# Spectral units as 28 operations each, emitted at the times of a table, in a single-core spectral and GEGLU kernel

## The chip, the cores and the metric

The kernel runs on one core of one Trainium2 chip. The core has a matrix engine (TensorE, PE in the profile; its weight loads are shown apart as PEld), VectorE (DVE), ScalarE (ACT), GpSimd (POOL) and SyncE (SP), which here issues all DMA transfers. Each engine works through its own list of instructions in order; between engines there are semaphores. The metric is the device time of one execution in microseconds (us), and for a kernel the median of its runs.

## What is computed

The input x is 8192 rows of 448 columns. It goes through two conditioned blocks:

```python
mod = (silu(c) @ w_mod)                      # six rows of 448: sa, ca, ga, sb, cb, gb
h = layernorm(x) * (1 + ca) + sa
x = x + ga * A(h)                            # spectral mixer
h = layernorm(x) * (1 + cb) + sb
x = x + gb * ((gelu(h @ w_gate) * (h @ w_up)) @ w_down)

def A(h):                                    # the transform is along the 8192 rows
    z = rfft(h)                              # 4097 frequencies x 448, as 4 blocks of 112
    h = relu(z @ w1 + b1)                    # complex, per block; relu on real and imaginary part
    o = h @ w2 + b2
    o = softshrink(o, 0.01)                  # real and imaginary part apart
    return irfft(o)
```

The matrix products need more precision than one pass of the matrix engine gives, so operands are split into a high and a low part and three products are added.

## The kernel before, in words

The program has three stretches.

1. **0 to about 80 us.** x is loaded, layer norm statistics are taken, and the first factor of the transform (128 points) runs on PE. Its result td goes to DRAM.
2. **About 80 to 419 us: the spectral stage**, which the change is about. There are 32 *units* (h, bt): h is a half of the columns (224 of 448), bt one of 16 groups of four frequencies. Each unit goes through the same operations, most of them twice (kk or p = 0, 1):
   - `fetch_t` (SP, L347 and L356): the unit's part of td into the tile tr, and for a new bt the factors s2. `split_t`: th on ACT and tl on POOL (helper lines L108 and L110 in the profile).
   - `stage_s2`: 12 matmuls (L378 to L380), zh on ACT (L386), zl on DVE (L387).
   - `stage_m1`: 12 matmuls (L424 to L429), hh on ACT (L441), hl on DVE (L442).
   - `stage_m2`: 12 matmuls (L451 to L456), the threshold t (p = 0 on DVE, L467; p = 1 on ACT, L465), y with four DVE operations (L477 or L479). `split_y`: yh on ACT (L108), yl on POOL (L110).
   - `stage_i1`: 3 matmuls (L508 to L510), us on ACT (L511); after both, two DMA stores into vd (L513).
3. **About 419 us to the end: GEGLU** over 32 chunks of 256 rows, with the second factor of the inverse transform at the start of each. PE is busy all through.

The order in stretch 2 is written out by hand. `step(i)` emits, one after the other: the fetch of unit i+2, s2 of unit i, the split of unit i+1, m2 of unit i-2, i1 of unit i-3, m1 of unit i-1. `step(0)` to `step(30)` follow each other, and `drain` writes out the rest. What an engine does follows this order, so the operations of one stage of one unit stand behind each other on each engine.

Side work for stretch 3 is hung into the steps with `at(i, hook, fn)`: a hook is one of five places in a step (load, pe, act, dve, pool). It loads and reduces modulation rows (`mod_sum`, L640 and L641; `mod_row`, L649), takes norms of the up-projection weights (`squares`, L672; `norms`, L681), sums the down-projection pieces (`down_sums`, L791 to L798), and, from step 18 on, splits gate and up weights into wh and wl (`weights_hi`, L770 to L773; `weights_lo`, L779 and L781) and the first down pieces (`down_hi`, L877; `down_lo`, L881). Short scalar work waits in a list `tiny`; `drip()` emits one entry of it between the operations of a unit.

On-chip tiles rotate: tr, s2, th, tl, t, y and us have two buffers, zh, zl, hh, hl, yh and yl four. Of the matrix engine's eight result banks, two each serve s2 (pa), m1 (pb), m2 (pc) and i1 with side work (pd).

Of the kernel before, what the change touches and what calls it, by code (L numbers as in the profile page):

```python
# [10 lines left out]
F32 = mybir.dt.float32  # L11
# [8 lines left out]
D = 448  # L20
# [18 lines left out]
LAM = 0.01  # L39
EPS = 1e-5  # L40
# [5 lines left out]
def spectral_geglu(ctx, tc, x, wt_in, wgu, wd, cvec, wmod, cf1, cs2, cmi, cgm, out):  # L46
# [290 lines left out]
    with ExitStack() as bctx:  # L337
# [21 lines left out]
        def split_t(h, bt, el=G):  # L359
            raw, s2 = trs.pop((h, bt))  # L360
            th = bp1.tile([128, GB, HC], F16, tag="th", name="th", bufs=2)
            tl = bp1.tile([128, GB, HC], F16, tag="tl", name="tl", bufs=2)
            split(th, tl, raw, el=el)
            tts[(h, bt)] = th, tl, s2

        cnt = {"z": 0, "h": 0}
        ctx_u = {}

        def stage_s2(h, bt):
            tht, tlt, s2 = tts.pop((h, bt))  # L370
            zs = []
            for kk in range(2):
                ps = bank("pa", "ps2")
                pv = ps.rearrange("p (r g k) -> p r g k", r=2, g=GB)
                for g in range(GB):
                    th = tht[:, g, kk * BS : (kk + 1) * BS]
                    tl = tlt[:, g, kk * BS : (kk + 1) * BS]
                    T.matmul(pv[:BS, :, g, :], th, s2[:, g, 0, :], start=True, stop=False)  # L378
                    T.matmul(pv[:BS, :, g, :], th, s2[:, g, 1, :], start=False, stop=False)
                    T.matmul(pv[:BS, :, g, :], tl, s2[:, g, 0, :], start=False, stop=True)  # L380
                zhi = zh[cnt["z"] % 4]
                cnt["z"] += 1
                zlo = bp.tile([BS, 2, ZW], F32R, tag="zl", name="zl", bufs=4)
                p3 = ps[:BS].rearrange("p (r q) -> p r q", r=2)
                c1 = ca1[:, 2 * h + kk : 2 * h + kk + 1]
                S.activation(zhi[:BS, :, 0 : GB * 64], p3, AF.Copy, scale=c1)  # L386
                V.scalar_tensor_tensor(  # L387
                    zlo[:, :, 0 : GB * 64], p3, c1, zhi[:BS, :, 0 : GB * 64].bitcast(F32), op0=ALU.mult, op1=ALU.subtract
                )
                if bt == 0:  # L390

                    z0 = bp.tile([BS, 1], F32, tag="z0", name="z0", bufs=2)
                    V.scalar_tensor_tensor(
                        z0, p3[:, 0, 0:1], c1, sa0[:, 2 * h + kk : 2 * h + kk + 1], op0=ALU.mult, op1=ALU.add
                    )
                    split(zhi[:BS, 0, 0:1], zlo[:, 0, 0:1], z0, eh=V.tensor_copy)
                    for z in (zhi, zlo):
                        z32 = z.bitcast(F32)
                        G.memset(z32[:BS, 0, ZW - 1 : ZW], 0.0)
                        G.memset(z32[:BS, 1, ZW - 2 : ZW], 0.0)  # L400
                        G.tensor_copy(z[:BS, 0, ZW - 2 : ZW - 1], z32[:BS, 1, 0:1])
                        G.memset(z32[:BS, 1, 0:1], 0.0)
                zs.append((zhi, zlo))
                drip()
            ctx_u[("z", h, bt)] = zs

        def stage_m1(h, bt):
            zs = ctx_u.pop(("z", h, bt))
            hs = []
            kr = 113  # L410
            w = ZW if bt == 0 else GB * 64
            for kk in range(2):
                k = 2 * h + kk
                zhi, zlo = zs[kk]
                if bt == 0:
                    banks = [bank("pb", "pm1a")[:BS, :w], bank(("pa", "pd")[kk], "pm1b")[:BS, :w]]
                else:
                    ps = bank("pb", "pm1")
                    banks = [ps[:BS, 0:w], ps[:BS, w : 2 * w]]
                for ro in range(2):  # L420

                    a, c = (0, 2) if ro == 0 else (1, 0)
                    o = banks[ro]
                    T.matmul(o, w1h[:kr, a, k, :], zhi[:kr, 0, :w], start=True, stop=False)  # L424
# [116 lines left out]
        def at(i, hook, fn, *args):  # L541
            side.setdefault((i, hook), []).append((fn, args))
# [783 lines left out]
```

## Time and profile before

| | |
|---|---|
| median of 3 runs | 1990.72 us (1990.11 to 1993.17) |
| profiled execution | 1993.32 us |
| its span | 1991.4 us |
| granted PE clock over the span | 0.982 |
| busy: PE, DVE, ACT, POOL | 1923.5, 1112.1, 789.9, 1209.0 us |

The span is the time from the first to the last instruction on record; the profiled execution's own time is 1.9 us longer. A share of busy time over the whole span mixes the three stretches, so the views are best cut at 84 and 418 us. A matmul's duration in the trace is from its issue to its modelled end, and matmuls overlap: what one costs PE is the distance from its start to the next one's.

### The profile page before, as it was taken

How to read it: one execution, taken by the hardware profiler on the slowest of the kernel's cores; microseconds unless marked ns; L12 is line 12 of the kernel's file. 1: busy time of each engine (PE TensorE's matmuls, PEld its weight loads, DVE VectorE, ACT ScalarE, POOL GpSimd, SP SyncE). 2: the span in 40 equal slices, each digit the busy share in tenths (PEclk: the TensorE clock that was granted, in tenths of full speed). 3: DMA queues.
4: the chain of work that ended last, by engine and by line, in shares of the span. 5: the costliest groups of instructions: out<-in, count | busy, mean ns of one | idle time of the engine just before them, and what ended most of it. 6: DMA issues, size and time to landing. Idle time of an engine off the chain costs nothing.

```text
span 1991.4 us, 43353 instructions
## 1 busy us (share of the span) xinstructions
PE 1923.5 (97%) x17622; PEld 1709.7 (86%) x17622; DVE 1112.1 (56%) x2320; ACT 789.9 (40%) x1334; POOL 1209.0 (61%) x1512
## 2 busy tenths in 40 slices
PE   7898989978999999999999999999999999999999
PEld 3588988957898888888888888988888988989898
DVE  7566777757555555555455555555555555555533
ACT  5576667734333333333333333333333333333322
POOL 3366556536666666666666666666666666666644
PEclk9888999979999999999999999999999999999999
DMA  9887757542111111111111111111111111111000
GB/s 348 293 281 220 243 148 207 156 126 63 48 43 43 43 43 45 49 42 42 54 43 42 43 42 43 47 46 42 42 42 43 42 43 43 43 43 43 21 17 20
DMA packets 147338, 165.74 MB, mean 83 GB/s; under 512 B 83889, under 2 KB 121521, under 8 KB 146754
## 3 DMA queue, kind: packets, MB, share of 16 engines
q1 hardware_dynamic: 147138, 162.97, 27.4%
q8 instruction: 138, 2.26, 0.5%
q14 instruction: 62, 0.51, 0.1%
HBM read 97.49 MB, written 49.66 MB: 74 GB/s over the span
## 4 chain that ended last, share of the span: by engine, by line
PE 81%; DVE 8%; ACT 4%; POOL 3%; issue 2%; DMA 1%; SPq 1%; ACTq 0%; DVEq 0%; POOLq 0%
PE pgu L1044 50%; PE pdn L1110 7%; PE pdn L1112 7%; PE pdn L1111 7%; PE ps L214 3%; DVE y L477 2%; DVE y L479 1%; DVE hl L442 1%; PE pi L944 1%; ACT t L465 1%; PE pi L942 1%; DMA tr<-td 1%; PE pi L943 1%; DVE zl L387 1%; ACT yh L108 1%
## 5 line engine op out<-in xcount | busy, mean ns | idle before, releaser
L1044 PE MATMUL pgu<-nt,wh 128*128 128x256 f16 x6272 | 833.8, 273 | 1.6 <-DVE nt L1035 1.6
L1044 PEld LDWEIGHTS <-wh 128*128 128x128 f16 x6272 | 602.5, 98 | 99.2 <-issue 31.7
L1080 ACT ACTIVATE gel<-pgu,dg 128x256 f32<-128x256 f32 x448 | 200.4, 473 | 795.2 <-PE pgu L1044 760.1
L1044 PE MATMUL pgu<-nt,wl 128*128 128x256 f16 (+1 forms) x3584 | 501.4, 272 | 0.1
L1110 PE MATMUL pdn<-wd,ac 128*128 128x224 f16 x1568 | 406.1, 259 | 2.0 <-ACT p L1139 2.0
L1112 PE MATMUL pdn<-wd,ac 128*128 128x224 f16 x1568 | 406.1, 259 | 0.2 <-DVE ac L1103 0.2
L1111 PE MATMUL pdn<-wd,ac 128*128 128x224 f16 x1568 | 406.1, 259 | 0.0
L1091 POOL TENSOR_TENSOR x<-x 128x128 f32<-128x128 f32 x223 | 242.2, 1086 | 235.0 <-DVE x L1085 235.0
L1103 DVE SCALAR_TENSOR_TENSOR ac<-x,sa_act,ac 128x896 f16<-128x896 f32 (+1 forms) x225 | 308.4, 1371 | 84.7 <-ACT ac L1102 84.7
L1044 PEld LDWEIGHTS <-wl 128*128 128x128 f16 (+1 forms) x3584 | 297.8, 97 | 57.2 <-issue 23.9
L1085 DVE TENSOR_TENSOR x<-pgu,gel 128x256 f32<-128x256 f32 x448 | 179.6, 418 | 284.9 <-ACT gel L1080 284.3
L1102 ACT ACTIVATE ac<-x,sa_act 128x896 f16<-128x896 f32 (+1 forms) x225 | 233.0, 1035 | 52.6 <-POOL x L1094 50.6
L1145 POOL TENSOR_TENSOR o<-u,p 128x224 f32<-128x224 f32 x32 | 21.1, 659 | 291.4 <-DVE u L1144 291.4
L1092 POOL TENSOR_TENSOR x<-x 128x128 f32<-128x128 f32 x223 | 160.1, 718 | 17.5
L1111 PEld LDWEIGHTS <-ac 128*128 128x128 f16 x1568 | 153.4, 98 | 2.5 <-issue 2.2
L1110 PEld LDWEIGHTS <-ac 128*128 128x128 f16 x1568 | 153.4, 98 | 0.6 <-issue 0.2
L1112 PEld LDWEIGHTS <-ac 128*128 128x128 f16 x1568 | 153.4, 98 | 0.5 <-DVE ac L1103 0.5
L110 POOL TENSOR_TENSOR yl<-y,yh 128x448 fp32r<-128x448 f32 x63 | 78.5, 1246 | 89.8 <-ACT yh L108 88.0
L1093 POOL TENSOR_TENSOR x<-x 128x128 f32<-128x128 f32 x223 | 114.8, 515 | 0.0
L1094 POOL TENSOR_TENSOR x<-x 128x128 f32<-128x128 f32 x223 | 107.6, 482 | 0.0
L110 POOL TENSOR_TENSOR tl<-tr,th 128x896 f16<-128x896 f32 x30 | 57.2, 1908 | 53.1 <-ACT th L108 52.2
L1124 POOL TENSOR_TENSOR o<-o,gb_r 128x448 f32<-128x448 f32 (+1 forms) x64 | 71.7, 1120 | 8.1 <-DVE o L1134 5.6
(294 smaller groups left out, 2854.3 us busy)
## 6 DMA issues: line engine op xcount, KB each, us to landing
tr<-td SPq DMA_DIRECT2D x64, 224.0 KB, 4.6
raw<-in_gu SPq DMA_DIRECT2D x28, 512.0 KB, 6.5
vd<-us SPq DMA_DIRECT2D x64, 224.0 KB, 2.9
xx<-in_x SPq DMA_DIRECT2D x32, 448.0 KB, 3.4
v<-vd SPq DMA_DIRECT2D x64, 224.0 KB, 2.9
out<-x SPq DMA_DIRECT2D x31, 448.0 KB, 2.6
nt<-pk SPq DMA_TRANSPOSE x480, 2.3
tb<-in_x SPq DMA_DIRECT2D x8, 896.0 KB, 17.7
```

The lines of the kernel that those rows point to most:

```text
L110: (el or V).tensor_tensor(lo, src, h, ALU.subtract)
L1044: T.matmul(pgu[i, t, q][:, pr * H : (pr + 1) * H], w[rows, tw, f0 : f0 + 128], nts[i][rows, tn, :], start=start, stop=stop, skip_group_che ...
L1080: S.activation(gl, ps[:, :H], AF.Gelu_apprx_tanh, scale=dg)
L1085: V.tensor_tensor(dst, ps[:, H : 2 * H].rearrange("p (b c) -> p b c", b=2), gl.rearrange("p (b c) -> p b c", b=2), ALU.mult)
L1091: e.tensor_tensor(s1, a21, a22, ALU.add)
L1092: e.tensor_tensor(s2, s1, a11, ALU.subtract)
L1093: e.tensor_tensor(s3, a11, a21, ALU.subtract)
L1102: S.activation(ac[:, 0, k], x[:, k], AF.Copy, scale=sc)
L1103: V.scalar_tensor_tensor(ac[:, 1, k], x[:, k], sc, ac[:, 0, k], op0=ALU.mult, op1=ALU.subtract)
L1110: T.matmul(ps, ac[:, 0, ka], wds[t][:, 0, kb], start=t == 0, stop=False)
L1111: T.matmul(ps, ac[:, 0, ka], wds[t][:, 1, kb], start=False, stop=False)
L1112: T.matmul(ps, ac[:, 1, ka], wds[t][:, 0, kb], start=False, stop=t == NP - 1)
```

## The change

Each unit becomes 28 operations. `AT` gives each of them a time in us, and unit i's operation is emitted at `i * STEP + AT[name]` with `STEP = 8.5`: all operations of all units and the side work go into one list of events, which is sorted by time and emitted in that order. The numbers only set the order of emission; nothing waits for a clock. A reader's time in the table lies behind its producer's by more than the producer takes: hh0 of a unit, for example, stands at 24.93 for matmuls that stand at 19.75, and m20, which reads hl1 of 27.85, at 34.0. Between s2 (12.75) and us (53.29) of one unit lie 40 us of table time, which is nearly five steps; before, a unit went from s2 to i1 in three steps (s2 in step i, m1 in i+1, m2 in i+2, i1 in i+3).

- The functions `split_t`, `stage_s2`, `stage_m1`, `stage_m2`, `split_y` and `stage_i1` are cut into one function for each engine's operation (`th_t`, `tl_t`, `s2_pe`, `z_hi`, `z_lo`, `m1_pe`, `h_hi`, `h_lo`, `m2_pe`, `t_op`, `y_op`, `y_hi`, `y_lo`, `i1_pe`, `us_op`). Their instructions are the same, but for the units with bt = 0: there the two extra columns of m1 become 12 small matmuls for each kk into a bank of pd, with a small Relu on ACT and a small operation on DVE right behind them.
- Half of the gate and up pieces (pr = 1, the up weights) were scaled on ACT, cast on ACT and subtracted on GpSimd. Now ACT scales and casts in one operation, GpSimd scales the raw piece in place (`weights_scale`), and subtracts a step later (`weights_sub`).
- The weight pieces' steps move by one, the three down pieces are four steps apart and not two, and four products of `all_max` are emitted together with the DVE operation that reads them.
- Buffer counts are as before. `step`, `m2_i1` and `drain` are gone.

On ACT, one step in the second half of the stage stood as follows before (zh, th, wh, yh, t, us and hh are the tiles of the list above; wh is a gate weight piece):

```order
L386 ACTIVATE zh_755<-ps_4350,ca_101 112x2x256
L386 ACTIVATE zh_756<-ps_4366,ca_101 112x2x256
L108 CAST th<-tr 128x896
L770 ACTIVATE wh<-raw,sw 128x4x256
L108 CAST yh<-y 128x448
L465 ACTIVATE t<-pm_4411,neglam 128x448
L511 COPY us<-pi_4432 128x448
L511 COPY us<-pi_4437 128x448
L108 CAST yh<-y 128x448
L441 ACTIVATE hh_761<-pm_4450 112x2x256
L441 ACTIVATE hh_762<-pm_4466 112x2x256
```

and stands now:

```order
L372 CAST th<-tr 128x896
L403 ACTIVATE zh_757<-ps_4508,ca_101 112x2x256
L403 ACTIVATE zh_758<-ps_4522,ca_101 112x2x256
L442 ACTIVATE hh_759<-pm_4486 112x2x256
L442 ACTIVATE hh_760<-pm_4542 112x2x256
L526 CAST yh<-y 128x448 x2
L549 COPY us<-pi_4567 128x448
L549 COPY us<-pi_4572 128x448
L778 ACTIVATE wh<-raw,sw 128x4x256
L492 ACTIVATE t<-pm_4601,neglam 128x448
```

Before, yh, t and yh of one unit stood around each other, each behind work of DVE on the one ahead. Now both yh follow each other a step after t, and th stands ahead of the zh of the unit before it.

At the start of the stage, ACT's rows before were

```order
L108 CAST th<-tr 128x896
L386 ACTIVATE zh_755<-ps_794,ca_101 112x2x256
L386 ACTIVATE zh_756<-ps_810,ca_101 112x2x256
L108 CAST th<-tr 128x896
L386 ACTIVATE zh_757<-ps_843,ca_101 112x2x256
L386 ACTIVATE zh_758<-ps_859,ca_101 112x2x256
L108 CAST th<-tr 128x896
L441 ACTIVATE hh_759<-pm_881 112x2x256
```

and are now

```order
L372 CAST th<-tr 128x896 x2
L403 ACTIVATE zh_755<-ps_796,ca_101 112x2x256
L403 ACTIVATE zh_756<-ps_809,ca_101 112x2x256
L372 CAST th<-tr 128x896
L403 ACTIVATE zh_757<-ps_856,ca_101 112x2x256
L403 ACTIVATE zh_758<-ps_869,ca_101 112x2x256
L442 ACTIVATE hh_759<-pm_840 112x2x256
L442 ACTIVATE hh_760<-pm_884 112x2x256
L680 ACTIVATE sq<-raw 128x1024
L648 ACTIVATE wm<-wm,cs 112x448 x4
```

th of unit 1 moved ahead of both zh of unit 0, and the four scalings of a modulation row (L648) now stand ahead of th of unit 3.

On POOL, two steps with an up piece between them were

```order
L781 TENSOR_TENSOR wl<-raw,wh 128x4x256
L110 TENSOR_TENSOR tl<-tr,th 128x896
L110 TENSOR_TENSOR yl<-y,yh 128x448 x2
L110 TENSOR_TENSOR tl<-tr,th 128x896
L110 TENSOR_TENSOR yl<-y,yh 128x448 x2
```

and are now

```order
L787 TENSOR_SCALAR raw<-raw,sw 128x1024
L379 TENSOR_TENSOR tl<-tr,th 128x896
L531 TENSOR_TENSOR yl<-y,yh 128x448 x2
L792 TENSOR_TENSOR wl<-raw,wh 128x4x256
L379 TENSOR_TENSOR tl<-tr,th 128x896
L531 TENSOR_TENSOR yl<-y,yh 128x448 x2
```

The scaling of the raw piece is new there; every step in this half has either it or the subtraction.

The core of the diff:

```diff
+STEP = 8.5
+AT = {
+    "fetch": -2.4, "th": 5.65, "tl": 8.01,
+    "s20": 12.75, "s21": 13.46, "zh0": 15.11, "zh1": 15.77, "zl0": 17.17, "zl1": 17.92,
+    "m10": 19.75, "m11": 22.67, "hh0": 24.93, "hh1": 25.53, "hl0": 27.17, "hl1": 27.85,
+    "m20": 34.0, "m21": 35.37, "t0": 37.03, "t1": 38.1, "y0": 39.06, "y1": 40.68,
+    "yh0": 43.1, "yh1": 43.7, "yl0": 45.07, "yl1": 46.23, "i10": 49.67, "i11": 50.34, "us0": 52.77, "us1": 53.29,
+    "load": 11.2, "act": 11.31, "dve": 12.16, "pool": 13.39, "pe": 14.15,
+}
...
-        def step(i):
-            def hook(name):
-                for fn, args in side.get((i, name), []):
-                    fn(*args)
-
-            if i + 2 < nu:
-                fetch_t(*units[i + 2])
-            hook("load")
-            hook("pe")
-            if i < nu:
-                stage_s2(*units[i])
-            if i + 1 < nu:
-                split_t(*units[i + 1], el=V if i < 1 else G)
-            hook("act")
...
+        def ev(t, fn, *args):
+            events.append((t, next(order), fn, args))
+
         def at(i, hook, fn, *args):
-            side.setdefault((i, hook), []).append((fn, args))
+            ev(i * STEP + AT[hook], fn, *args)
+
+        def run(until):
+            todo = sorted((e for e in events if e[0] < until), key=lambda e: e[:2])
+            events[:] = [e for e in events if e[0] >= until]
+            for _, _, fn, args in todo:
                 fn(*args)
...
+        stages = {"s2": s2_pe, "zh": z_hi, "zl": z_lo, "m1": m1_pe, "hh": h_hi, "hl": h_lo, "m2": m2_pe}
+        stages.update({"t": t_op, "y": y_op, "yh": y_hi, "yl": y_lo, "i1": i1_pe, "us": us_op})
+        for i, u in enumerate(units):
+            if i > 1:
+                at(i, "fetch", fetch_t, *u)
+            if i > 0:
+                at(i, "th", th_t, *u)
+                at(i, "tl", tl_t, *u, V if i == 1 else G)
+            for name, fn in stages.items():
+                for kk in range(2):
+                    extra = (V,) if name == "yl" and kk and i == nu - 1 else ()
+                    at(i, f"{name}{kk}", fn, *u, kk, *extra)
...
+            if bt == 0:
+
+                px = bank("pd", "pmx")
+                sl = slice(ZW - 2, ZW)
                 for ro in range(2):
+                    mlp1(px[:BS, 2 * ro : 2 * ro + 2], z, ro, k, sl)
+                pv = px[:BS, :4].rearrange("p (r q) -> p r q", r=2)
+                S.activation(hhi[:BS, :, sl], pv, AF.Relu)
+                h_lo_of(hhi, hlo, pv, sl)
...
         def weights_hi(pr, j):
-            raw = raws[("w", pr, j)]
+            assert ready
             fs = slice(pr * F + j * 256, pr * F + (j + 1) * 256)
-            if pr == 0:
-                S.activation(wh[:, :, fs], raw, AF.Copy, scale=sw[:, pr : pr + 1])
-            else:
-                S.activation(raw, raw, AF.Copy, scale=sw[:, pr : pr + 1])
-                S.copy(wh[:, :, fs], raw)
+            S.activation(wh[:, :, fs], raws[("w", pr, j)], AF.Copy, scale=sw[:, pr : pr + 1])
...
+        def weights_scale(pr, j):
+            raw = raws[("w", pr, j)]
+            G.tensor_scalar(raw, raw, sw[:, pr : pr + 1], None, op0=ALU.mult)
...
         for j in range(14):
-            at(17 + j, "load", pre, fp, ("w", j % 2, j // 2), load_w, j % 2, j // 2)
-            at(18 + j, "act", weights_hi, j % 2, j // 2)
-            at(18 + j, "dve", weights_lo, j % 2, j // 2)
+            pr, jj = j % 2, j // 2
+            at(18 + j, "load", pre, fp, ("w", pr, jj), load_w, pr, jj)
+            at(19 + j, "act", weights_hi, pr, jj)
+            if pr == 0:
+                at(20 + j, "dve", weights_lo, pr, jj)
+            else:
+                at(19 + j, "pool", weights_scale, pr, jj)
+                at(20 + j, "pool", weights_sub, pr, jj)
...
-        for i in range(17, nu - 1):
-            step(i)
-        drain()
+        run(1e9)
```

More of the change, by code (lines that the diff above doesn't have):

```diff
@@ L1 @@
+import itertools
 import math
@@ L364, in split_t @@
             tts[(h, bt)] = th, tl, s2
         cnt = {"z": 0, "h": 0}
[L367 to L386, printed above, removed]
+        st = {}
@@ new lines, in s2_pe @@
+        def s2_pe(h, bt, kk):
+            tht, tlt, s2 = tts[(h, bt)]
+            ps = bank("pa", "ps2")
+            pv = ps.rearrange("p (r g k) -> p r g k", r=2, g=GB)
+            for g in range(GB):
+                th = tht[:, g, kk * BS : (kk + 1) * BS]
+                tl = tlt[:, g, kk * BS : (kk + 1) * BS]
+                T.matmul(pv[:BS, :, g, :], th, s2[:, g, 0, :], start=True, stop=False)
+                T.matmul(pv[:BS, :, g, :], th, s2[:, g, 1, :], start=False, stop=False)
+                T.matmul(pv[:BS, :, g, :], tl, s2[:, g, 0, :], start=False, stop=True)
+            if kk:
+                del tts[(h, bt)]
+            st[("s", h, bt, kk)] = ps
@@ L499, in stage_i1 @@
[L499 to L516 removed]
+            el.tensor_tensor(yl, st.pop(("y", h, bt, p)), st[("yh", h, bt, p)].bitcast(F32), ALU.subtract)
@@ new lines, in y_lo, with i1_pe @@
+            st[("yl", h, bt, p)] = yl
+        def i1_pe(h, bt, p):
+            yh, yl = st.pop(("yh", h, bt, p)), st.pop(("yl", h, bt, p))
+            ps = bank("pd", "pi1")
+            parts = [(0, 0, 1), (1, 1, 2)] if bt == 0 and p == 0 else [(1, 0, 2)]
+            for m, lo, hi in parts:
+                o = ps[:, lo * HC : hi * HC]
+                T.matmul(o, mih[:, m, :], yh[:, lo:hi], start=True, stop=False)
+                T.matmul(o, mih[:, m, :], yl[:, lo:hi], start=False, stop=False)
+                T.matmul(o, mil[:, m, :], yh[:, lo:hi], start=False, stop=True)
+            st[("i", h, bt, p)] = ps
@@ new lines, in us_op @@
+        def us_op(h, bt, p):
+            if p == 0:
+                st[("u", h, bt)] = bp.tile([128, GB, HC], F32, tag="us", name="us", bufs=2)
+            us = st[("u", h, bt)]
+            S.copy(us[:, 2 * p : 2 * p + 2, :], st.pop(("i", h, bt, p))[:, :D].rearrange("p (g c) -> p g c", g=2))
+            if p:
+                for ro in range(2):
+                    dma(
+                        vd[h, :, ro * 64 + bt * GB : ro * 64 + (bt + 1) * GB],
+                        us[ro * 64 : ro * 64 + 64],
+                    )
@@ L829, in spectral_geglu @@
         at(16, "pe", scales2)
-        for i in range(1, 17):
-            step(i)
+        run(17 * STEP + AT["load"] - 0.5)
         nctx.close()
```

242 lines of the change are left out of this document (101 added, 141 removed).

## The prediction

> **What bounds the kernel now.** I read the stages first. The change touches only the spectral stage, whose 32 units run from about 84 to 418 us; what follows it is one long PE-bound stretch. The busy time of each engine in the whole stage and its two halves (columns: stretch, length, PE, PEld, DVE, ACT, POOL busy with counts, granted clock, DMA share, GB/s):
>
> ```profile
> 84.00:418.00 334.00, 304.88 (x2626) 289.03 (x2626) 235.76 (x493) 229.00 (x381) 193.22 (x190) 0.93 0.69 204
> 84.00:250.00 166.00, 152.62 (x1342) 144.53 (x1343) 110.92 (x239) 109.11 (x186) 100.36 (x118) 0.91 0.79 244
> 250.00:418.00 168.00, 152.26 (x1286) 144.50 (x1285) 124.84 (x256) 119.89 (x195) 92.86 (x72) 0.95 0.59 164
> ```
>
> PE looks full, but a busy PE at a low clock is not full. So I read what a unit costs PE at full clock. In the timeline of one step I take the first matmul of each stage (i1, m1, a side product, s2, m2, the next i1):
>
> ```profile
> 221.82 0.38 PE L508 MATMUL pi<-yh,mih 128*128 128x448 f32 x1
> ...
> 223.06 0.28 PE L424 MATMUL pm<-zh,w1h 113*112 113x256 f32 x1
> ...
> 225.95 0.60 PE L681 MATMUL pw<-onesb,sq 128*128 128x1 bf16 x8
> ...
> 226.48 0.26 PE L378 MATMUL ps<-s,th 128*112 128x128 f16 x1
> ...
> 227.84 0.35 PE L451 MATMUL pm<-w2h,hh 113*128 113x224 f32 x1
> ...
> 230.59 0.38 PE L508 MATMUL pi<-yh,mih 128*128 128x448 f32 x1
> ```
>
> From start to start: i1 1.24, m1 2.89, s2 1.36, m2 2.75, together 8.24 us a unit, and 0.53 for the side product. Against that stands the pace. Unit 0's ScalarE threshold t starts at 97.9, unit 31's at 413.3 (first row below); 14 of the 32 start before 250 (second row), the last of them at 241.53, and the last but one of all at 408.09:
>
> ```profile
> L465 ACT ACTIVATE t<-pm,neglam x32: 627/629/635, 97.9 to 413.3; 128x448 f32<-128x448 f32 x32
> ...
> L465 ACT ACTIVATE t<-pm,neglam 128x448 f32<-128x448 f32 x14 | 8.8, 630 | 0.0
> ...
> 241.53 0.64 ACT t L465
> ...
> 408.09 0.64 ACT t L465
> ```
>
> So the first 13 steps took 143.6 us, 11.05 each; the next 17 took 166.6, 9.80 each. PE needs 8.24. The waits of the three other engines in the stage say why:
>
> ```profile
> DVE y L477 <- ACT t L465: 43.0, 32, 2.5
> DVE hl L442 <- ACT hh L441: 30.6, 20, 3.4
> ...
> ACT yh L108 <- DVE y L479: 48.0, 24, 7.3
> ACT yh L108 <- DVE y L477: 27.3, 30, 1.7
> ...
> POOL yl L110 <- ACT yh L108: 88.0, 56, 7.4
> ```
>
> Each engine waits for the one before it in the same unit: t, y, yh, yl and hh, hl stand directly behind each other in program order. No engine is full; the chain of dependent operations inside one step is the bound. Without side work that chain repeats exactly every 8.98 us (the chain of waits: hl, three steps running), and whatever is inserted on any engine lengthens it:
>
> ```profile
> 227.09 1.29 DVE hl L442 x2
> ...
> 236.07 1.29 DVE hl L442 x2
> ...
> 245.05 1.29 DVE hl L442 x2
> ```
>
> There is a second loss. PE's gaps pull its clock down (one-microsecond stretches):
>
> ```profile
> 323.00:324.00 1.00, 0.48 (x2) 0.30 (x2) 1.00 (x1) 1.00 (x3) 1.00 (x1) 1.00 0.92 244
> 324.00:325.00 1.00, 0.10 (x1) 0.10 (x1) 0.97 (x3) 1.00 (x3) 1.00 (x1) 1.00 0.94 297
> ...
> 326.00:327.00 1.00, 1.00 (x7) 1.00 (x6) 0.84 (x3) 0.92 (x1) 1.00 (x1) 0.50 0.97 232
> 327.00:328.00 1.00, 1.00 (x7) 1.00 (x7) 0.90 (x2) 0.00 (x0) 1.00 (x2) 0.50 1.01 200
> ```
>
> A stretch with some 1.4 us idle in two was followed by half clock, 7 matmuls a microsecond. Over the stage the clock of 0.93 is worth (1 - 0.93) x 334 = 23 us.
>
> **The change part by part.** *The order.* A unit's 28 operations are emitted at the times of a table, 8.5 us apart per unit, so on every engine another unit's work stands between a producer and its reader. The table's 8.5 is above PE's 8.24, and the other engines hold it: from 250 on, ACT has 119.89 / 18 = 6.7 us a unit and DVE 124.84 / 18 = 6.9; before 250 each has about 110 us for 14 to 16 units, 6.9 to 7.9. So PE sets the pace, if nothing is late.
>
> Late half: PE's 8.24, and stalls. I put these at 0.4 a step, since ACT and DVE still meet single operations that no slot of the table fits (a down-projection piece, the four products that now reduce on DVE right behind PE). Bounds: 8.24, and today's 9.80. I take 8.65, nearest to PE, because a stall needs a delay larger than the 1.4 to 5 us that the table puts in front of each reader.
>
> Early half: PE has the side product of 0.53 a step and 8 modulation matmuls of 0.54, 0.3 a step over 13. That makes 9.07. ACT has the four modulation scalings, 4 x 0.655 = 2.6 us in one piece, in four steps:
>
> ```profile
> L649 PE MATMUL psm<-wm,onec 112*128 112x448 f32 x8 | 3.7, 538 | 0.0
> ...
> L640 ACT ACTIVATE wm<-wm,cs 112x448 f32<-112x448 f32 x16 | 9.4, 655 | 0.0
> ```
>
> VectorE and GpSimd wait behind that, and units 8 and 9 (bt = 0) put a small Relu on ACT that waits for PE at once. I allow 0.45 a step and take 9.5; the bounds are 9.07 and today's 11.05.
>
> *The fill.* ACT's first rows now hold th of unit 1 ahead of zh of unit 0:
>
> ```profile
> 78.61 0.94 ACT L108 CAST th<-tr 128x896 f16<-128x896 f32 x1 [3.15 <-DMA tr<-td]
> 82.08 0.69 ACT L386 ACTIVATE zh<-ps,ca 112x512 fp32r<-112x512 f32 x1 [2.53 <-PE ps L380]
> ...
> 83.95 0.93 ACT L108 CAST th<-tr 128x896 f16<-128x896 f32 x1
> ```
>
> The first zh can start at 83.95 + 0.93 = 84.9, not 82.08: 2.8 us. PE also does m1 of unit 1 (2.89) before the first m2. So the first t comes at 97.9 + 5.7, about 104; bounds 98 and 108 (ACT's 2.6 us of scalings now stand ahead of unit 3's th).
>
> *The drain.* In steady state s2 to t of one unit is 25.35 us in the table; in the fill it is about 23. At the end PE has, from s2 of unit 31 to its m2: s2 1.36, m1 of 30 (second half) 1.44, i1 three times 3.7, m1 2.89, m2 three times 8.25, 17.7 us. That shortens the last distance by 5.5. So the last t starts at 104 + 13 x 9.5 + 18 x 8.65 - 5.5 = 377.7. Behind it today come 418.79 - 413.3 = 5.5 us until the last store goes out, through y, yh, yl, i1 and us:
>
> ```profile
> 418.79 2.85 DMA vd<-us
> ```
>
> I take 6.5, as y of unit 30 is closer ahead on DVE now. That is 384.2 against 418.8: 34.6 us less. The stretch behind it, from this store on, has the same instructions and keeps its length.
>
> *The up-projection weights.* ACT loses a scaling and a cast that read each other (1.16 + 1.05) and does one 1.18 operation; GpSimd gets the scaling, a form that it does not run today. Rows: 128 columns take 0.658, 448 take 1.42.
>
> ```profile
> L770 ACT ACTIVATE wh<-raw,sw 128x1024 f16<-128x1024 f32 x5 | 5.9, 1176 | 0.0
> ...
> L772 ACT ACTIVATE raw<-raw,sw 128x1024 f32<-128x1024 f32 x5 | 5.8, 1161 | 0.0
> L773 ACT CAST wh<-raw 128x1024 f16<-128x1024 f32 x5 | 5.2, 1046 | 0.2
> ...
> L209 POOL TENSOR_SCALAR fr<-f,y 128x128 f32<-128x128 f32 x46 | 29.5, 658 | 35.6 <-DVE y L196 33.3 <-PE ps L214 2.3
> L900 POOL TENSOR_SCALAR gb_r<-gb_r,ds_d 128x448 f32<-128x448 f32 x1 | 1.4, 1420 | 0.0
> ```
>
> 1024 columns are then between 1.42 + 576 x 0.00238 = 2.8 and 1.42 x 1024 / 448 = 3.25 us. POOL has 92.86 / 18 = 5.2 us a unit in this half; 3.25 in every second makes 6.8. That hides under PE's 8.24. If it did not, at most 7 x 3.25 = 23 us would come on the path.
>
> The sum against the profiled execution is 1993.32 - 34.6 = 1958.7 us. That execution is 2.6 us above the median of the three runs, so 1956.
>
> The Trainium skill ("TensorE: Matmul & The Clock Gate", the clock-gate part) says that the clock halves only after an idle window of about 3.4 us. The rows above disagree: two thirds of two microseconds were enough. By the rule the new order's small stalls would cost no clock, and of the 13 us of stalls in my sum perhaps 6 would go: 1950.
>
> **The rivals.** *PE is the bound throughout*: the slack takes up every side operation. 104 + 13 x 9.07 + 18 x 8.24 - 5.5 + 6.5 = 371.2, 47.6 less: 1943. For it: no engine is full; against it: ACT's 2.6 us pieces exceed most slacks.
>
> *The early half keeps its pace.* The transfers bound it:
>
> ```profile
> DMA packets 17125, 40.55 MB, mean 244 GB/s; under 512 B 1771, under 2 KB 10004, under 8 KB 16724
> ...
> tr<-td SPq DMA_DIRECT2D x32, 224.0 KB, 5.4
> ```
>
> 40.55 MB in 166 us, at a share of 0.79; at 9.5 a step the same bytes need some 275 GB/s. If they do not come, 13 x 1.55 = 20 us of the gain go: 1976. Against it: ACT waited for a tile of td once in the stage, the 3.15 in the row above.
>
> *Slower: the coupled order falls into step with a late transfer.* th of unit i+1 stands ahead of zh of unit i on ACT, and the stores of an earlier unit stand ahead of the next fetch on SP; ACT feeds all others. From fetch to th the table has 8.05 us; today the two or three issues (0.6 each) and the landing need 1.8 + 4.6, at most 1.8 + 7.8:
>
> ```profile
> DMA to landing us min/median/max: 3.4/4.6/7.8
> ```
>
> With some 3 us of slack behind th, landings of about 9 us would begin to stop PE each step; at 11, the pace becomes about 10.4 in both halves, and the end 104 + 31 x 10.4 - 5.5 + 6.5 = 427.4: 8.6 more, 1999. It turns slower from 10.1 a step. Landings are half of that now.
>
> **How the numbers follow.** The forecast 0.54, PE-bound throughout 0.20, early half unchanged 0.14, slower 0.08, and 0.04 for gains and losses that cancel. Faster is 0.54 + 0.20 + 0.14 = 0.88; within 0.2%, which is about what a measurement of this kernel tells from no change (4 us), 0.04; slower 0.08. The range goes from 1940, below the PE bound by 3 us for a shorter fill, to 1978, above the second rival.
>
> **What would show it.** In the changed profile: t about 9.5 us apart up to unit 13 and 8.65 behind; waits of DVE for ACT's t and hh, of POOL for ACT's yh and of ACT for y below a third of those above, PE's waits instead on few single places; half-clock stretches mainly in the fill and drain; the last store of us at about 384; the GpSimd scaling at 2.8 to 3.25. I am wrong if t stays over 10 apart, if ACT's th waits for tr in many steps, or if the stretch behind the last store changes its length.

## The result and the profile after

| | before | after |
|---|---|---|
| median of the runs | 1991.61 us (1990.11 to 1993.17) | 1964.38 us (1961.44 to 1966.44) |
| ratio, 95% interval | | 0.9862 [0.9845, 0.9879], that is 27.2 us less |
| profiled execution, its span | 1993.32, 1991.4 us | 1964.53, 1962.4 us |
| granted PE clock over the span | 0.982 | 0.990 |

The forecast was 1956 with a range from 1940 to 1978. The time lies 8 us above the forecast and inside its range. The sum of the prediction can be checked term by term in the trace after. First the two halves of the spectral stage, cut at 234 us, shortly ahead of unit 13's t (columns: stretch, length, busy time of PE, PEld, DVE, ACT and POOL with counts, granted clock, DMA share, GB/s):

```profile
84.00:234.00 150.00, 139.15 (x1290) 132.27 (x1291) 100.47 (x219) 100.57 (x173) 93.20 (x113) 0.95 0.87 260
234.00:390.00 156.00, 149.97 (x1385) 145.82 (x1383) 135.42 (x274) 120.37 (x201) 121.54 (x84) 1.00 0.66 186
```

The late half has a full clock and PE 96% busy, the early half has neither. The ACT threshold t and the stores of us, from the views of these two lines (after the colon: shortest, median and longest in ns, then the first and the last start in us):

```profile
L492 ACT ACTIVATE t<-pm,neglam x32: 613/634/667, 99.1 to 382.8; 128x448 f32<-128x448 f32 x32
L552 SPq DMA_DIRECT2D vd<-us x64: 445/538/1237, 116.2 to 390.0; - x64
```

The start of t of unit 13 is 237.60 in ACT's timeline. So the terms come out as follows; the last column adds up to 5.8, the distance between 384.2 and 390.0:

| term | forecast | measured | difference |
|---|---|---|---|
| first t | 104 | 99.1 | -4.9 |
| steps 0 to 13 | 123.5 (9.5 each) | 138.5 (10.65 each) | +15.0 |
| steps 13 to 31, with the drain | 150.2 | 145.2 | -5.0 |
| last t to last store | 6.5 | 7.2 | +0.7 |
| last store | 384.2 | 390.0 | +5.8 |
| last store to the end of the span | unchanged, 1572.6 | 1572.4 | -0.2 |

Two terms that came out 5 us below the forecast hide most of one that came out 15 above, so it is in good part luck that the total lies near the forecast. The distances from one t to the next in us, worked out from its starts in ACT's timeline, show where the 15 us lie:

```
before, early  11.7 11.3  9.0 11.2 10.7 14.7 12.2 12.3 10.6 11.2 10.8  9.0  9.0
after,  early   9.0 12.2  7.4  8.8 15.1 15.9 14.0 11.4  7.4 10.1  9.6  8.7  8.7
before, late   10.8  9.1 12.1  9.5  8.8  9.2  8.9 10.0  9.9 10.4  9.8 10.5  9.6  9.5  8.9 11.9  7.6  5.2
after,  late    8.7  8.4  8.5  8.4  8.2  8.4  8.2  9.1  7.2  8.2  8.2  9.3  7.0  8.2  8.2  9.0  5.9  6.0
```

From unit 4 to 7 the new order is slower than the old one, and only from unit 11 on does it run at PE's price. The waits between 80 and 395 us (columns: engine and line that waited, what it waited for, total, times, longest; rows left out at the marks) have changed their places:

```profile
...
POOL yl L531 <- ACT yh L526: 19.7, 15, 3.8
POOL wm L649 <- ACT wm L648: 18.3, 4, 6.7
ACT hh L463 <- PE pmx L438: 18.2, 4, 8.3
ACT t L492 <- PE pm L480: 15.2, 20, 1.6
...
DVE hl L445 <- ACT hh L463: 12.2, 4, 4.7
...
ACT th L372 <- DMA tr<-td: 11.2, 8, 2.4
...
ACT yh L526 <- DVE y L508: 8.4, 6, 2.3
PE pm L433 <- DVE hl L445: 7.3, 5, 3.1
...
ACT wm L648 <- DMA wm<-in_mod: 4.9, 3, 2.4
```

POOL's wait for yh fell from 88.0 to 19.7, ACT's for y from 75.3 to about 10, DVE's 43.0 for t is no longer on the list. In their place stand operations of the modulation rows (wm) and of the two extra columns in units 8 and 9 (pmx; the hh of L463 is the small Relu), and these exist in the early half only.

The worst place is at 150 to 166 us. ACT's timeline there (start, duration, engine, line, operation; in brackets the idle time before it and what ended it; rows left out at the marks):

```profile
149.40 2.35 ACT L648 ACTIVATE wm<-wm,cs 112x448 f32<-112x448 f32 x4 [1.50 <-DMA wm<-in_mod]
151.65 0.61 ACT L492 ACTIVATE t<-pm,neglam 128x448 f32<-128x448 f32 x1
152.16 0.92 ACT L372 CAST th<-tr 128x896 f16<-128x896 f32 x1
...
157.23 0.96 ACT L549 COPY us<-pi 128x448 f32<-128x448 f32 x2
166.53 0.17 ACT L463 ACTIVATE hh<-pmx 112x4 fp32r<-112x4 f32 x1 [8.34 <-PE pmx L438]
```

And POOL's:

```profile
151.82 2.13 POOL L649 TENSOR_TENSOR wm<-wm 112x896 f32<-112x896 f32 x1 [3.89 <-ACT wm L648]
153.91 1.13 POOL L531 TENSOR_TENSOR yl<-y,yh 128x448 fp32r<-128x448 f32 x1
155.02 1.42 POOL L563 TENSOR_SCALAR sb_r<-sb_r,sk 128x448 f32<-128x448 f32 x1
156.42 1.41 POOL L563 TENSOR_SCALAR cb_r<-cb_r,sk 128x448 f32<-128x448 f32 x1
157.79 1.89 POOL L379 TENSOR_TENSOR tl<-tr,th 128x896 f16<-128x896 f32 x1
```

And DVE's:

```profile
155.07 1.60 DVE L508 SCALAR_TENSOR_TENSOR y<-pm,t 64x224 f32<-64x224 f32 x4 [3.25 <-POOL yl L531]
156.70 0.75 DVE L411 SCALAR_TENSOR_TENSOR zl<-ps,ca,zh 112x512 fp32r<-112x512 f32 x1
...
157.80 1.90 DVE L120 TENSOR_TENSOR zl<-z,zh 112x1 fp32r<-112x1 f32 x1
159.62 0.74 DVE L411 SCALAR_TENSOR_TENSOR zl<-ps,ca,zh 112x512 fp32r<-112x512 f32 x1
...
160.79 1.28 DVE L445 SCALAR_TENSOR_TENSOR hl<-pm,hh 112x512 fp32r<-112x512 f32 x2
```

And PE's:

```profile
161.53 0.56 PE L433 MATMUL pm<-zh,w1h 113*112 113x256 f32 x1 [3.09 <-DVE hl L445]
...
164.22 0.21 PE L433 MATMUL pmx<-zh,w1h 113*112 113x2 f32 x1
...
166.16 0.33 PE L438 MATMUL pmx<-zh,w1l 112*112 112x2 f32 x1
```

Read from the top, this is one chain. A modulation row is not there when ACT comes to it; ACT waits for it 1.50 us and scales it for 2.35. POOL has waited 3.89 for that and takes its sum (2.13) ahead of yl. DVE's y waits 3.25 for yl, and both zl and then hl stand behind y in DVE's order, one of them behind a one-column operation that took 1.90 us. PE's m1 waits 3.09 for hl. By then the clock is half (from 160.19 us on), and the twelve two-column matmuls pmx take 2.1 us; ACT, which stands in line at the small Relu, is idle for 8.34 us and with it everything that ACT feeds.

### The profile page after: what moved, and what is told of

Its sections match the earlier page's. It is cut to its first block, busy times and chain, and to the rows that moved or that the text cites. A ratio compares the mean times of both kernels' runs of the same rounds, so it can differ in the third digit from the quotient of the medians.

```text
span 1962.4 us, 43447 instructions
## 1 busy us (share of the span) xinstructions
PE 1909.1 (97%) x17670; PEld 1700.0 (87%) x17670; DVE 1113.1 (57%) x2320; ACT 782.0 (40%) x1327; POOL 1229.2 (63%) x1519
## 4 chain that ended last, share of the span: by engine, by line
PE 76%; DVE 2%; POOL 1%; ACT 0%; issue 0%; DMA 0%; SPq 0%; POOLq 0%; ACTq 0%
PE pgu L1057 52%; PE pdn L1125 7%; PE pdn L1123 7%; PE pdn L1124 7%; PE pi L957 1%; PE pi L955 1%; PE pi L956 1%; DVE ac L1116 0%; POOL x L1105 0%; DVE n L1007 0%; DVE n L1006 0%; ACT ac L1115 0%; POOL x L1104 0%; DVE cst L975 0%; DMA vd<-us 0%
## 5 line engine op out<-in xcount | busy, mean ns | idle before, releaser
L1057 PEld LDWEIGHTS <-wh 128*128 128x128 f16 x6272 | 602.4, 98 | 99.1 <-issue 31.7
L1105 POOL TENSOR_TENSOR x<-x 128x128 f32<-128x128 f32 x223 | 159.7, 716 | 17.5
L531 POOL TENSOR_TENSOR yl<-y,yh 128x448 fp32r<-128x448 f32 x63 | 72.5, 1163 | 20.5 <-ACT yh L526 19.7
```

Source lines behind the costliest of these rows:

```text
L1057: T.matmul(pgu[i, t, q][:, pr * H : (pr + 1) * H], w[rows, tw, f0 : f0 + 128], nts[i][rows, tn, :], start=start, stop=stop, skip_group_che ...
L1105: e.tensor_tensor(s2, s1, a11, ALU.subtract)
```

## The experiments

The expectations call the theories by letters. A: the small Relu of the extra columns holds up ACT, which works in order. B: the transfers of the early half bound it. C: the modulation rows' loads stand in SP's queue, hold up the next fetch of tr, and ACT waits for tr. D: side work stands on the engines' lists, GpSimd's above all, and holds up the work of the units behind it. E: the two-column matmuls themselves cost PE time and clock. F and G, for the last run, are explained there. Times of the kernel before stand beside each, from the same chip and set of runs; a 95% interval of the ratio stands where there were several.

### Undo the waits alone (A and C)

**e1_edge**: the extra columns' matmuls, Relu and subtraction become events of their own, for both kk together.

```diff
+    "xp": 21.2, "xh": 23.55, "xl": 23.6,
...
+            if u[1] == 0:
+                for name, fn in (("xp", x_pe), ("xh", x_hi), ("xl", x_lo)):
+                    at(i, name, fn, *u)
```

> The two extra columns of units 8 and 9 (bt = 0): their 24 small matmuls, Relu and subtraction are emitted at times of their own (21.2, 23.55, 23.6), and no longer inside m1, where ACT stands behind PE. Theory A (ACT's four waits of 18.2 us in all for these matmuls were the lost part of the early half): t of units 4 to 8 comes some 10 us apart and not 15.1, 15.9, 14.0, 11.4, the kernel is 12 to 18 us faster than the changed kernel, 1946 to 1952 us. Theory B (transfers bound the early half; ACT's th waited 11.2 us for tr and landings reach 10.2 us): ACT waits for tr instead, under 4 us gained, 1960 to 1964.

**e2_rows**: load and scalings of a modulation row at other places of the step.

```diff
-            at(n, "dve", pre, npool, key, load_mod_row, q)
-            at(n + 1, "dve", mod_sum, key)
+            at(n, "pe", pre, npool, key, load_mod_row, q)
+            at(n + 1, "pool", mod_sum, key)
```

> Only the modulation rows move: the load of the next row is emitted behind the matmul that frees its one buffer, not ahead of it, and the four scalings stand behind t and not ahead. Theory C (SP's queue stood 12.7 us behind such loads and held the next fetch; ACT then waited for tr): SP no longer waits for psm for long, ACT's wait for tr falls from 11.2 to under 5 us, 3 to 8 us faster than the changed kernel, 1956 to 1961. Theory B (bandwidth): tr stays late, within 2 us of 1964.

**e3_both**: both edits.

> Both edits. A and C together: 15 to 24 us faster than the changed kernel, 1940 to 1949, unit 0 to unit 13 in about 120 us where it was 138.5 (the forecast of 9.5 a step would be 123.5). Theory B: the early half stays above 130 us, and the kernel above 1955.

Measured, before at 1991.8: e1 1963.59 us (0.9862 [0.9847, 0.9877]), e2 1963.69 (0.9855 [0.9838, 0.9872]), e3 1962.58 (0.9850 [0.9834, 0.9867]); the change itself has 0.9862 [0.9845, 0.9879]. The first 13 steps took 137.2, 137.3 and 138.3 us against 138.5. None gains, where 12 to 18, 3 to 8 and 15 to 24 us were expected. In e1 the Relu's wait shrank from 18.2 to 7.0 us, but ACT's wait for tr rose from 11.2 to 14.7 (80 to 395 us) and one step of 17.4 us remained. A alone falls. In e2 the row's load still waited 11.5 us on SP for the matmul of the row before (12.7 in the changed kernel, with the tr fetch queued behind it), and ACT's wait for tr, which was to fall under 5 us, rose from 11.2 to 21.5. The row's scalings came 7.7 us of table time behind the load, less than the 8.5 before. So e2 did not take away what C names, and C is neither shown nor refuted by it.

### The weights apart from the order

**e4_before_weights**: the old order, with the new split of the up weights.

```diff
-                S.activation(raw, raw, AF.Copy, scale=sw[:, pr : pr + 1])
-                S.copy(wh[:, :, fs], raw)
+            S.activation(wh[:, :, fs], raws[("w", pr, j)], AF.Copy, scale=sw[:, pr : pr + 1])
...
+                G.tensor_scalar(raw, raw, sw[:, pr : pr + 1], None, op0=ALU.mult)
```

> The old order with the new split of the up weights alone (ACT one operation and not two, the scaling on GpSimd right ahead of the subtraction). If the order is what made the late half faster: ACT's t comes about 1 us earlier in seven steps, 3 to 7 us faster than before, 1984 to 1988. If ACT's double operation was the late half's problem: 12 us or more faster, under 1980. If GpSimd's added 3 us stand in front of tl and yl in the old order: not faster at all.

**e12_old_scale**: the reverse, the changed kernel with the old scaling and cast on ACT and no scaling on GpSimd.

> The changed kernel with the old split of the up weights (two operations on ACT, no scaling on GpSimd). With the slack of the new order ACT's extra 1 us in every second step is hidden (ACT 6.7 + 1 under PE's 8.24): steps 18 to 30 stay at 8.3 to 8.5, within 3 us of 1964. If the weights' part carries the late half: 8.9 or more a step, 6 to 10 us slower, 1970 to 1974.

e4: 1992.16 us against 1991.8, ratio 1.0005 [0.9993, 1.0016]. e12: 1966.76 against 1989.06, 0.9885 [0.9868, 0.9903]; its late half took 146.0 us against 145.2. e4 came out as the last of its three cases, not faster at all; that GpSimd's added work is the reason is not shown. The intervals of e12 and of the change overlap: in the new order the new split of the weights may be worth 2.4 us (by the medians), 4.6 (by the ratios) or nothing. Nearly all of the gain is the order's.

### Which side work costs the early half

**e5_raw_once**: the first of the norms' pieces is loaded and read for all 14, 6.8 MB less.

```diff
-            at(1 + n, "load", pre, npool, ("n", pr, j), load_w, pr, j)
+            if n == 0:
+                at(1, "load", pre, npool, ("n", 0, 0), load_w, 0, 0)
```

> The changed kernel, but the norms' 14 loads of weight pieces are one: the squares all read the first piece (so the norms, and with them the scales, are those of that piece). 13 x 512 KB less to move between about 84 and 234 us, every engine's work unchanged. Theory B (the transfers' bandwidth makes tr, m and the modulation rows late): ACT's wait for tr falls below 3 us and unit 0 to unit 13 takes 10 us or more less than 138.5. Theory D (GpSimd's list holds side work in front of yl, which waits in order for other engines): under 4 us less.

**e6_no_rows**: the four modulation rows become constants.

```diff
-        for n, (key, q, dst) in zip((1, 4, 7, 10), (("cb", 4, cb_r), ("sb", 3, sb_r), ("ga", 2, ga_r), ("gb", 5, gb_r))):
-            at(n, "dve", pre, npool, key, load_mod_row, q)
-            at(n + 1, "dve", mod_sum, key)
-            at(n + 2, "act", mod_sum2, key)
-            at(n + 3, "pe", mod_row, key, dst)
+        for r in (cb_r, sb_r, ga_r, gb_r):
+            G.memset(r, 0.05)
```

> The changed kernel without the four modulation rows (loads, the 16 scalings on ACT, the sums on GpSimd, the matmuls; constants stand in their place): ACT 10 us, GpSimd 13 us, PE 4 us and 3.2 MB less. Theory D: the wait of GpSimd for ACT's scalings (18.3 us) and SP's wait for psm (12.7 us) go with it, unit 0 to unit 13 takes 10 us or more less. Theory B: 3 to 5 us less, since it is only a tenth of the bytes.

**e7_no_down**: no down-projection sums in the early half, with their loads and stores.

```diff
-        for t, n in enumerate((2, 3, 5, 6, 9, 11, 12)):
-            at(n, "load", pre, npool, ("m", t), load_m, t)
-            at(n + 1, "dve", down_sums, t)
-            at(n + 2, "load", store_m, t)
+        V.memset(dn, 0.5)
```

> The changed kernel without the down pieces' sums in the first half (loads, four GpSimd sums each, one reduction on DVE, stores; the later loads read the plain weights instead): GpSimd 18.6 us, DVE 7.6 us and 8.6 MB less. Theory D: 6 us or more less, since GpSimd's sums stand ahead of yl and wait for the load (4.7 us). Theory B: 10 us or more, as it takes away a fifth of the bytes.

Single executions beside one of before at 1992.56 us:

| | time | steps 0 to 13 | steps 13 to 31 |
|---|---|---|---|
| the change | 1964.38 (median) | 138.5 | 145.2 |
| e5, norms' loads 14 to 1 | 1963.65 | 136.0 | 145.2 |
| e6, no modulation rows | 1950.98 | 126.8 | 145.2 |
| e7, no down sums | 1968.33 | 137.1 | 149.1 |

B falls: 6.8 MB less in e5, and in e7 the down pieces' bytes and 18.6 us of POOL work less, shorten the early half by 2.5 and 1.4 us, where B had put 10 or more for each; with one execution of each, such differences are not clear of noise. With e7 D falls for the down sums too, for which it had put 6 us. For the modulation rows D's size came: without them, though they have few bytes, 11.7 us of the early half go. C's path is not the way: ACT's wait for tr did not fall with the rows but rose, from 8.5 to 17.2 us between 80 and 240 us. Half clock fell from 13.3 to 3.4 us of the 13 steps, which by my estimate (half of the difference) is up to 4.9 of the 11.7.

What the rows' work waits for, the view of the tile wm shows in the changed kernel and in the kernel before (scalings on ACT, then issues on SP, first and last start):

```profile
L648 ACT ACTIVATE wm<-wm,cs x16: 651/654/712, 93.0 to 192.4; 112x448 f32<-112x448 f32 x16
L642 SPq DMA_DIRECT2D wm<-in_mod x4: 328/334/612, 84.2 to 182.8; - x4
```

```profile
L640 ACT ACTIVATE wm<-wm,cs x16: 651/652/666, 100.7 to 206.2; 112x448 f32<-112x448 f32 x16
L634 SPq DMA_DIRECT2D wm<-in_mod x4: 530/537/623, 88.6 to 193.7; - x4
```

Taken row by row from the traces, the first scaling of a row started 12.1, 9.2, 14.7 and 10.7 us behind the issue of its load in the old order. The three landings on record took 7.0, 7.0 and 7.3 us and were over by then; ACT never waited. Both orders set the scalings one step behind the load. Now the distances are 8.8, 6.4, 9.4 and 8.0 us, the landings on record 8.8, 6.0 and 5.6 (none for the third row), and ACT waited for three of the four rows, 4.9 us in all. A shorter step has uncovered a transfer that the longer one hid. But that is not the whole of it: POOL's wait for ACT's scalings grew from 4.4 to 18.3 us, and at most 4.9 of these can be the landing. No run separates the landing from where the operations stand, so it is not shown that the landing is the cause of the 11.7 us.

### The two-column matmuls (E)

**e9_no_side_edge**: e5, e6, e7 and e1's edit together. **e10_no_side_no_x**: also without the extra columns' matmuls, Relu and subtraction.

```diff
             if u[1] == 0:
-                for name, fn in (("xp", x_pe), ("xh", x_hi), ("xl", x_lo)):
-                    at(i, name, fn, *u)
+                at(i, "xp", x_none, *u)
```

> All three left out, and the two extra columns of units 8 and 9 at times of their own. If the side work, by whatever way, is what the early half lost: unit 0 to unit 13 takes 13 x 8.3 to 8.8 = 108 to 114 us (138.5 in the changed kernel), the kernel about 1936 to 1942. If the units themselves hold the early half (units 8 and 9, the fill's clock): above 120.

> The kernel with the norms' single load, no modulation rows and no down sums, and without the 48 small matmuls, the Relus and the subtractions for the two extra columns of units 8 and 9 (constants stand there). There, with the small matmuls, units 6 to 9 still came 11.1, 13.9, 10.0, 10.0 us apart and the clock halved at 165 us though PE never waited. Theory E (matmuls of two columns cost PE 0.1 us each and count as idle for the clock): the clock stays at full through units 5 to 10, unit 0 to unit 13 takes 112 to 116 us (122.4 with them). If the clock's fall there came from something else: above 119.

e9 1953.91 us, e10 1941.73, one execution each (before: 1992.56 and 1989.06). The first 13 steps took 122.4 and 114.9 us. So e9 missed the 108 to 114 that the side work alone would have given, and e10 hit theory E's 112 to 116; e10's are nearly all 8.7 (7.6, seven of 8.7, 10.0, 10.0, 8.8, 8.7, 8.7). The first and the last of the 24 two-column matmuls of one unit in e9's PE timeline:

```profile
160.94 0.17 PE L434 MATMUL px<-zh,w1h 113*112 113x2 f32 x1
...
163.13 0.24 PE L439 MATMUL px<-zh,w1l 112*112 112x2 f32 x1
163.23 0.24 PE L393 MATMUL ps<-s,th 128*112 128x128 f16 x1
```

24 in 2.29 us, 0.095 each. And what came behind them, two-microsecond stretches of e9:

```profile
160.00:162.00 2.00, 2.00 (x22) 2.00 (x20) 1.85 (x5) 1.23 (x2) 1.64 (x2) 1.00 1.13 347
162.00:164.00 2.00, 2.00 (x28) 2.00 (x29) 0.00 (x1) 0.24 (x2) 1.19 (x1) 1.00 0.73 247
164.00:166.00 2.00, 2.00 (x26) 1.94 (x24) 0.68 (x5) 1.82 (x3) 0.00 (x0) 0.65 0.70 154
166.00:168.00 2.00, 2.00 (x11) 2.00 (x11) 1.94 (x5) 0.05 (x1) 0.00 (x0) 0.50 0.01 3
168.00:170.00 2.00, 2.00 (x7) 1.78 (x6) 1.83 (x3) 1.90 (x4) 0.77 (x1) 0.50 0.00 0
```

and of e10:

```profile
164.00:166.00 2.00, 2.00 (x24) 2.00 (x23) 1.37 (x4) 1.46 (x2) 0.12 (x1) 1.00 1.08 301
166.00:168.00 2.00, 2.00 (x30) 1.80 (x29) 0.00 (x0) 1.53 (x3) 1.77 (x1) 1.00 0.80 251
```

In e9 PE is never idle there and the clock is halved from 164.6 to 171.4; in e10 no stretch between fill and end is at half clock. So the extra columns cost 7.5 us of the early half: 2 x 2.3 of PE time and about 3 of clock (half of 6.8 us at half clock). e9's late half has one more half-clock stretch at 335 us and a step of 13.1; e2, e7 and e10 have a step of 11 to 12 at the same place. I did not pursue it.

### A better kernel

**e11_spread** keeps all work. It sets the small Relu and subtraction of the extra columns later, cuts a row's work into five events at different places of the steps, and moves the down sums and the row scalings.

```diff
+    "xh0": 23.55, "xh1": 25.52, "xl0": 23.6, "xl1": 25.6,
+    "tl2": 16.6, "load": 11.2, "act": 11.31, "dve": 12.16, "pool": 13.39, "pe": 14.15,
...
+            at(n, "pe", pre, npool, key, load_mod_row, q)
+            at(n + 1, "pool", mod_scale, key)
+            at(n + 1, "tl2", mod_sum, key)
+            at(n + 2, "pool", mod_sum2, key)
+            at(n + 3, "act", mod_row, key)
+            at(n + 3, "pe", mod_out, key, dst)
```

> The changed kernel with its side work where no engine waits for it: the Relu and subtraction of the extra columns 4 us behind their matmuls, the modulation rows' loads behind the matmul that frees their buffer, scalings, sums, matmul and copy each at a time of its own, the down sums behind both yl, the row scales in step 14 and not 7. Theory D (in-order waits of side work): GpSimd's wait for ACT's scalings falls from 18.3 to under 6 us, SP's for psm from 12.7 to under 3, unit 0 to unit 13 takes 118 to 128 us (138.5), the kernel 10 to 20 us faster than the changed kernel, 1944 to 1954. If only the amount of the side work counts, and not where it stands: within 4 us of 1964.

**e13_wide** is e11 with m1 of units 8 and 9 in 258 columns, as in the old order: one half of the result in a bank of pb, the other in one of pd, and no two-column matmul.

```diff
+            if bt == 0:
+                px = bank("pd", "px")
+                mlp1(ps[:BS, :ZW], z, 0, k, slice(0, ZW))
+                mlp1(px[:BS, :ZW], z, 1, k, slice(0, ZW))
```

> The kernel with the spread side work, and in units 8 and 9 m1 with 258 columns as in the old order: the real half goes to a bank of pb and the imaginary half to a bank of pd, with one Relu and one subtraction for each half at the places where the two-column ones stood. The 48 two-column matmuls (2.4 us a unit at full clock) are gone, nothing is left out. Theory E (these 48 matmuls cost their time and, while they run, count as idle for the clock): units 4 to 9 lose the half-clock stretch at 154 to 171 us and the 18.7 us step; the first 13 steps take 121 to 126 us (133.3 with the two-column matmuls), and the time falls by 7 to 12 us, to 1948 to 1953. Theory F (the stalls of units 4 to 8 come from the modulation rows and the order of the lists, the two-column matmuls only lie in the same place): 13 steps stay at 130 to 134 us, time 1957 to 1960. Theory G (the wide result holds a pd bank for which i1 then waits): PE waits of 2 to 3 us in front of pi in units 8 and 9, 13 steps at 127 to 131, time 1953 to 1957.

e11 1959.5 us (1958.26 to 1962.51), 0.9851 [0.9836, 0.9867], against 1989.06; 13 steps in 133.3. It missed its 1944 to 1954 us and 118 to 128: POOL's wait for the scalings is off the list, but the interval overlaps that of the change, so that spreading the side work alone is no gain clear of noise. e13 1952.77 us (1951.35 to 1953.45), 0.9804 [0.9790, 0.9817], against 1992.96; 13 steps in 125.9. Theory E had given 121 to 126 and 1948 to 1953, F and G smaller gains; i1 waited 0.4 us at most in these units, where G had put 2 to 3. The interval lies below those of the change and of e11: the wide matmuls are worth 7.4 us of the early half, where e9 and e10 had shown 7.5. Much of it is clock: half clock fell from 17.1 to 3.4 us of the 13 steps. And e13 is the fastest of the kernels that keep all the work, 40 us below before. Its remaining stall in the early half is the modulation row again, in ACT's, POOL's and PE's timelines:

```profile
147.61 2.35 ACT L666 ACTIVATE wm<-wm,cs 112x448 f32<-112x448 f32 x4 [3.74 <-DMA wm<-in_mod]
```

```profile
150.86 1.89 POOL L380 TENSOR_TENSOR tl<-tr,th 128x896 f16<-128x896 f32 x1 [7.48 <-ACT th L373]
```

```profile
155.55 0.34 PE L434 MATMUL pm<-zh,w1h 113*112 113x258 f32 x1 [4.19 <-POOL zl L427]
```

ACT stands before the row's scalings for 3.74 us; th, tl and POOL's edge operations on zl behind them come late, and PE waits 4.19. An earlier load of the row was not tried.

## Why the prediction was right or wrong

**PE's price: right.** 8.24 + 0.53 = 8.77 us a step without the modulation matmuls; e10, which has no stalls to speak of, ran most of its steps at 8.7 (114.9 / 13 = 8.84 in the mean). In the late half the first 16 steps were 8.33 each.

**The early half: this is the term that failed.** "I allow 0.45 a step" measured (138.5 - 13 x 9.07) / 13 = 1.6 a step. The step had named the right two suspects, ACT's scalings and the small Relu, and mis-sized both. First, the 48 two-column matmuls had no term of their own on PE: 2 x 2.3 us, and more at half clock (the twelve pmx of the lines above start 0.18 apart in the mean). Before, the two columns rode in 258-column matmuls, 0.28 us long and 0.12 apart, the same as those with 256. Second, the scalings were priced by their own 2.6 us and not by the transfer in front of them; I had set the landing time of tr against the new pace, and not that of wm. By the runs the 138.5 are made up so: PE's 13 x 8.77 = 114.0 (e10: 114.9), the extra columns 7.5 (e9 less e10), the modulation rows 11.7 (e6), of which their matmuls, 3.9, were priced; some 5 us are left for the norms' loads, the down sums and what the parts do to each other. These parts come from single executions of different kernels, so the sum is an estimate.

**The late half: right in mechanism, the stalls set too high.** 0.4 a step was allowed, 8.33 - 8.24 = 0.1 measured; "PE is the bound throughout" (8.24) was nearer there. The drain gave 2 x 8.24 - 5.9 - 6.0 = 4.6 us against 5.5 forecast.

**The first t: wrong by 5 us.** "The first zh can start at 83.95 + 0.93" took the old start of the second th for the time at which it can start. It had stood behind both zh, not waited for its tile. ACT's timeline after:

```profile
80.65 0.94 ACT L372 CAST th<-tr 128x896 f16<-128x896 f32 x1 [0.88 <-DMA tr<-td]
82.30 0.69 ACT L403 ACTIVATE zh<-ps,ca 112x512 fp32r<-112x512 f32 x1 [0.71 <-PE ps L394]
```

The th ran in ACT's idle time and zh moved by 0.22 us, not by 2.8. The second term, 2.89 for m1 of unit 1, went the same way: before, PE waited 1.60 and 0.66 us at s2 of unit 1, now m1 fills such time, and the first matmul of m2 starts at 93.82 us against 93.55. The first t came 1.2 us later than before, and ACT had by then waited 2.45 us for the first modulation row.

**The weights.** GpSimd's scaling was put at 2.8 to 3.25 us:

```profile
L787 POOL TENSOR_SCALAR raw<-raw,sw x7: 2843/3659/3828, 271.5 to 369.5; 128x1024 f32<-128x1024 f32 x7
```

3.66 at the median, above the upper bound of two rows scaled by columns. It hid as forecast: POOL has 121.54 / 18 = 6.75 us a unit (6.8 forecast), and e12 shows no cost.

**The clock.** "By the rule the new order's small stalls would cost no clock" was the other side of it, and the rows stay against the rule of the Trainium skill ("TensorE: Matmul & The Clock Gate", the clock-gate part): in the changed kernel half clock begins at 160.2, 1.7 us into a PE gap of 3.1, and in e9 with no gap at all. The forecast that half clock would remain mainly in fill and drain held but for this one stretch, 10.2 us long. (The fill's lasted from 98.8 to 102.2.)

**The rivals.** PE throughout (1943) did come in the late half, and e10, without the side work and the extra columns, ran at 1941.73. "The early half keeps its pace" was nearest in size, 10.65 against 11.05 a step, but its reason fell: the early half moved 260 GB/s, more than the 244 before, and e5 and e7 show that fewer bytes do not help. The slower rival did not come: the landings of tr grew from 4.6 to 5.7 us at the median, the longest to 10.2, and ACT waited for tr 11.2 us in all, 8 times, at most 2.4 us.

**The signs.** The prediction called itself wrong if t stayed over 10 us apart: in the early half it did (10.65 in the mean). Of the waits that were to fall below a third, DVE's for hh fell from 30.6 to 12.2 only, all of it at the small Relu. The last store came at 390 and not at 384. The waits of DVE for t, of POOL for yh and of ACT for y fell as far as was said.

**What stays open:** how much of the rows' 7.8 us beyond their matmuls is their landing, how much their operations on ACT and POOL and how much clock, since no run loaded them earlier; the one long step in the late half of some kernels; and whether the wide matmuls would gain as much without the spread side work, which no run tried.

## What to carry to other kernels

When an order gets faster, set every transfer's landing time against the new distance from its issue to its reader, the rare side loads first: an engine that works in order and waits for one of them holds up everything behind it. Price small matmuls by a start-to-start distance, not by their columns, and where some columns can ride in a larger matmul, leave them there. Read the start of an instruction that never waited as where it stood in its list, not as when its data came.

## What the runs showed of the hardware

- A two-column f32 matmul with 112-column weights costs nearly as much as one with 256 columns: 0.095 us from start to start against 0.12 (e9; its m1 starts at 159.51 and 159.63). The weight load of 112 columns takes 177 ns beside it in e9, overlapping the matmul before.
- The granted clock fell to a half although PE issued without a gap (e9, 164.6 to 171.4), after 24 such matmuls; without them (e10) it did not. Of e9's two sets of 24 only one was followed by half clock. Half-clock stretches come in multiples of 3.4 us (3.4, 6.8, 10.2, 17.1 and more), and counted back in such steps from 164.6 a border lies at 161.2, so that this set had 2.0 us in one window, while the other (149.90 to 152.2) was cut by the border at 150.95. The Trainium skill ("TensorE: Matmul & The Clock Gate", the clock-gate part) gives a free-running window of 3413 ns, which fits.
- The kept traces say how much is enough. I counted, in windows of 3.413 us set by the borders of the half-clock stretches, from 110 to 375 us of all fourteen traces, the time in which PE was idle or in two-column matmuls. Of 972 windows at full clock with less than 1.1 us of it none was followed by half clock, of 16 with 1.1 to 1.5 us two, of 37 with more 33. In the kernel before, the idle time of the window ahead of a half-clock stretch is 1.4 to 1.9 us six times and 2.6 once. With no idle time at all, two-column matmuls of 2.0 us in e9 and of 2.1 in e3 were followed by half clock, 2.0 us of them in e1 were not. That they count as idle fits these counts; why one of them went the other way stays open.
- A one-column DVE operation with both operands in SBUF took 1.90 us beside a GpSimd operation, and 0.16 otherwise. In the changed kernel (the view of its line):

```profile
L120 DVE TENSOR_TENSOR zl<-z,zh x4: 159/160/1903, 157.8 to 176.9; 112x1 fp32r<-112x1 f32 x4
```

The long one started at 157.80, 0.01 us behind POOL's tl, and both ended at 159.7 (lines above). In e13 another took 1.03 us and ended with POOL's sum of wm. The Trainium skill ("SBUF — State Buffer", the part on who interferes with whom) says that such an operation and one of GpSimd that reads SBUF share a port pair which the first holds for its whole length; these rows agree.
